# A causal convolution moved from a split between TensorE and VectorE to sixteen small TensorE tiles, in a fused retention and gated-linear-unit kernel

## The chip, the cores and the metric

The kernel runs on one core of one Trainium2 chip. The metric is device time in microseconds (us) of one execution. In the profile PE is TensorE (PEld its weight loads), DVE is VectorE, ACT is ScalarE, POOL is GpSimd and SP is SyncE, which here only issues DMAs.

## The reference

q, k and v are 8 batches x 8 heads x 576 positions x 64. First comes a retention layer, which is attention with a fixed decay in place of softmax; then a gated linear unit with a causal convolution as its gate:

```python
scores = scale * np.matmul(q, k.transpose(0, 1, 3, 2))
gamma = 1.0 - 2.0 ** (-5.0 - np.arange(H, dtype=np.float32))
Dmat = np.where(rel >= 0, gamma[:, None, None] ** rel[None, :, :], 0.0)
x = np.matmul(scores * Dmat[None], v)      # then heads side by side: (8, 576, 512)
for k in range(5):
    gate_pre += conv_w[k][None, None, :] * xp[:, k:k + S, :]   # xp: x with 4 zeros ahead
gate = 1.0 / (1.0 + np.exp(-gate_pre))
out = (gate * (x @ w_val)) @ w_out
```

The convolution is per channel: each of the 512 channels has its own five taps and is mixed with no other.

## The kernel before, in words

The sequence is cut into chunks of 128 positions, so a batch has four chunks and 64 positions left over. Two batches make a unit `u`; their leftovers are joined in one chunk of 2 x 64. That gives nine steps to a unit, and with four units 36 steps (L126 to L131).

A step `s` of attention is `load` (L135: q and k as float32 by SP's queue, v cast to bf16 on the way by POOL's queue), `cast` (L153: POOL multiplies q and k with the decay factors and rounds them to bf16), `transp` (L162: eight PE transposes into `tp`, then DVE copies `qt` and ACT copies `kt`), `scores` (L174: PE, then DVE multiplies with the mask into `am`), `state` (L193: PE, then ACT copies the running state `w`) and `attn_out` (L214: PE, then ACT copies the result into `xt`, the layer's x with channels on partitions, 512 channels as four tiles of 128, with four zero columns ahead). Loads run four steps ahead and casts two.

When a batch is done, `push_block` (L247) puts the gated unit's work for a block of positions on the list `work`: four `conv(d)`, one for each tile of channels; four `val(d)`; and one `outp(m)` for each 128 positions. There are 13 blocks: seven of 512 columns, two of 256, four of 2 x 64. The main loop (L320) takes three or four items off that list in each step, between the parts of attention; what is left runs after the last step. This gives the order in which the program is written; a scheduler then sets the final order on each engine, and each engine executes its own instructions in order.

`conv(d)` at L261 has two forms. For the channel tiles 0 and 1 (`PE_DT`), PE multiplies a 128x128 diagonal matrix of the weights of one tap with the shifted window of `xt`, ten times a tile: five taps, and for each the bf16 weight and its rounding remainder (L268). ACT applies the sigmoid from PSUM (L270). For the tiles 2 and 3, DVE does one multiply (L272) and four multiply-adds (L274), and ACT applies the sigmoid in place (L276). `val(d)` at L279 is four matmuls with `wval` (L284), then DVE multiplies with the gate into `zt` (L289). `outp(m)` at L291 is four matmuls with `wout` (L294), an ACT copy to `ob` (L297) and a DMA from SP's queue.

PSUM has eight banks: one for `tp` (pool `tpp`), two for the scores, one each for the attention output and the state, and three in the pool `glp`, which `cps`, `vps` and `ops` share in turn. SBUF pools: six buffers each for the loaded q, k and v, four each for their casts, four for `ob`.

Of the kernel before, what the change touches and what calls it, by code (L numbers as in the profile page):

```python
# [14 lines left out]
F32 = mybir.dt.float32  # L15
BF16 = mybir.dt.bfloat16
# [11 lines left out]
def kernel(  # L28
# [10 lines left out]
    nc = tc.nc  # L39
# [11 lines left out]
    lng = [math.log(1.0 - 2.0 ** (-5.0 - h)) for h in range(H)]  # L51
    PE_DT = (0, 1)

# [50 lines left out]
    wval = cst.tile([P, DT, DM], BF16)  # L104
    wout = cst.tile([P, DT, DM], BF16)
    diag = cst.tile([P, len(PE_DT), KC, 2, P], BF16)
    cwh = cst.tile([P, KC, DT], BF16)
    cwl = cst.tile([P, KC, DT], F32)

    def load_weights():  # L110
# [7 lines left out]
        nc.vector.tensor_copy(cwh, cw)  # L118
        nc.vector.tensor_tensor(cwl, cw, cwh, op=ALU.subtract)
        for n, dt_ in enumerate(PE_DT):  # L120
            for kk in range(KC):
                nc.vector.tensor_scalar_mul(diag[:, n, kk, 0, :], ident, cw[:, kk, dt_:dt_ + 1])
                nc.vector.tensor_scalar_mul(diag[:, n, kk, 1, :], ident, cwl[:, kk, dt_:dt_ + 1])

# [10 lines left out]
    def load(s):  # L135
        u, bb, c = steps[s]
        r = st.setdefault(s, {})
        qf = ld.tile([P, H, D], F32)
        kf = ld.tile([P, H, D], F32)
        vb = ld.tile([P, H, D], BF16)  # L140
        if bb is None:
            for x in range(2):
                b = 2 * u + x
                sl = slice(x * REM, (x + 1) * REM)
                for dst, src, eng in ((qf, q, nc.sync), (kf, k, nc.sync), (vb, v, nc.gpsimd)):
                    eng.dma_start(out=dst[sl], in_=src[b, :, NC * P:S, :].rearrange("h p d -> p h d"))
        else:
            b = 2 * u + bb
            for dst, src, eng in ((qf, q, nc.sync), (kf, k, nc.sync), (vb, v, nc.gpsimd)):
                eng.dma_start(out=dst, in_=src[b, :, c * P:(c + 1) * P, :].rearrange("h p d -> p h d"))  # L150
        r.update(qf=qf, kf=kf, vb=vb)

    def cast(s):  # L153
# [5 lines left out]
        nc.gpsimd.tensor_tensor(kb, r["kf"], fk[:, c, :].unsqueeze(2).to_broadcast([P, H, D]), op=ALU.mult)  # L159
        r.update(qb=qb, kb=kb)  # L160
# [86 lines left out]
    def push_block(u, bb, t0, n):  # L247
# [12 lines left out]

        def conv(d):  # L261
            gt = gl.tile(shape, F32, tag=f"g{N}", name="gt")
            if d in PE_DT:
                cp = glp.tile(shape, F32, tag="gps", name="cps")
                i = PE_DT.index(d)
                for kk in range(KC):
                    for p2 in range(2):
                        nc.tensor.matmul(cp, lhsT=diag[:, i, kk, p2, :], rhs=win(d, kk),  # L268
                                         start=(kk == 0 and p2 == 0), stop=(kk == KC - 1 and p2 == 1))
                nc.scalar.activation(gt, cp, AF.Sigmoid)  # L270
            else:
                nc.vector.tensor_scalar_mul(gt, win(d, 0), cw[:, 0, d:d + 1])  # L272
                for kk in range(1, KC):
                    nc.vector.scalar_tensor_tensor(gt, in0=win(d, kk), scalar=cw[:, kk, d:d + 1], in1=gt,  # L274
                                                   op0=ALU.mult, op1=ALU.add)
                nc.scalar.activation(gt, gt, AF.Sigmoid)  # L276
            g[d] = gt

        def val(d):  # L279
# [3 lines left out]
            for do in range(DT):  # L283
                nc.tensor.matmul(vp, lhsT=wval[:, do, d * P:(d + 1) * P], rhs=win(do, PAD),  # L284
                                 start=(do == 0), stop=(do == DT - 1))
# [17 lines left out]

        for d in range(DT):
            work.append((conv, d))
        for d in range(DT):
# [73 lines left out]
```

## Time and profile before

| what | value |
|---|---|
| median of 3 runs | 245.89 us (245.19 to 252.98) |
| the profiled execution's own time | 246.88 us |
| its span, first to last instruction | 245.2 us |
| mean granted PE clock | 0.95 |
| DMA, mean rate over the span | 140 GB/s |
| first matmul starts / last one ends | 18.1 / 240.5 us |

A row of a group reads: line, engine, operation, output<-inputs, shapes, count | busy us in all, mean ns of one | idle time of the engine just ahead of these, and what ended it. A row of waits reads: who waited <- for whom: us in all, times, longest. A row of the chain that ended last reads: start in us, us, what. A row of the timeline reads: start in us, us covered, what, count. A row of windows gives for a stretch its length, then busy us and instruction count for PE, PEld, DVE, ACT and POOL, then the granted clock, the DMA share and GB/s. Matmuls are pipelined, so the mean of one (its latency) is longer than the distance from one to the next.

### The profile page before, as it was taken

Reading aid. Unit: us, or ns where it says so; the run is one execution under the profiler, and the core shown is the slowest. Engines: PE = TensorE matmul, PEld = TensorE weight load, DVE = VectorE, ACT = ScalarE, POOL = GpSimd, SP = SyncE. Lnnn points to the kernel's source line nnn. Section 1 sums busy time; section 2 is a strip of 40 time slices with the busy share of each in tenths; the row PEclk is TensorE's granted clock in tenths of the full one; section 3 lists DMA queues with packets and bytes.
Section 4 is the critical chain, followed back from the end, with each engine's and each line's share of the span. In section 5 each row is a group of like instructions: output and inputs, shape, how many; then the busy total and the mean of one; then the engine's idle time right before and its main releaser. Section 6 shows DMA issues by size and latency. Waiting matters only on the chain.

```text
span 245.2 us, 4666 instructions
## 1 busy us (share of the span) xinstructions
PE 190.4 (78%) x1732; PEld 109.4 (45%) x1732; DVE 165.1 (67%) x323; ACT 109.8 (45%) x242; POOL 112.0 (46%) x126
## 2 busy tenths in 40 slices
PE   0007899259997989849978989759969999699592
PEld 0005564124554654415444745425534745356371
DVE  2073579994694582994895672992993854963991
ACT  2024465043634754534444755336445743533451
POOL 8129999624547392814444574706345620000000
PEclk9999999858999999989999999959999999979999
DMA  9999999903999999991997999935634901004032
GB/s 116 189 167 209 241 206 238 205 3 21 240 177 207 211 234 111 221 214 11 264 218 112 235 237 171 155 87 92 122 24 75 159 5 45 0 19 155 15 118 82
DMA packets 121478, 34.39 MB, mean 140 GB/s; under 512 B 115824, under 2 KB 116848, under 8 KB 121456
## 3 DMA queue, kind: packets, MB, share of 16 engines
q1 hardware_dynamic: 80256, 28.32, 47.4%
q0 software_dynamic: 38560, 5.77, 32.7%
q10 hardware_dynamic: 2640, 0.01, 0.7%
q8 instruction: 13, 0.21, 0.4%
q14 instruction: 9, 0.07, 0.1%
HBM read 30.42 MB, written 9.44 MB: 163 GB/s over the span
## 4 chain that ended last, share of the span: by engine, by line
PE 64%; DVE 18%; issue 7%; ACT 5%; POOL 4%; DVEq 0%; POOLq 0%
PE cps L268 15%; PE ops L294 14%; DVE gt L274 13%; PE vps L284 9%; PE tp L167 8%; PE o L226 7%; PE sc L183 6%; PE o L236 3%; DVE am L186 3%; ACT gt L276 2%; PE sts L202 2%; POOL vb L150 1%; ACT kt L171 1%; ACT w L209 1%; DVE gt L272 1%
## 5 line engine op out<-in xcount | busy, mean ns | idle before, releaser
L274 DVE SCALAR_TENSOR_TENSOR gt<-xt,cw,gt 128x512 f32<-128x512 bf16 (+2 forms) x104 | 67.2, 717 | 0.0
L158 POOL TENSOR_TENSOR qb<-qf,fq 128x512 bf16<-128x512 f32 x36 | 37.7, 1048 | 38.4 <-PE tp L167 19.3
L284 PE MATMUL vps<-xt,wval 128*128 128x512 bf16 (+2 forms) x208 | 39.8, 328 | 11.5 <-DVE zt L289 11.5
L186 DVE TENSOR_TENSOR am<-sc,mask_c 128x512 bf16<-128x512 f32 x64 | 41.2, 682 | 9.1 <-PE sc L183 8.9
L150 POOL DMA_DIRECT2D vb<-in_v_dram x32 | 29.6, 927 | 35.8 <-PE o L226 23.8
L170 DVE COPY qt<-tp 128x512 bf16<-128x512 bf16 x36 | 15.2, 421 | 42.3 <-PE tp L167 42.3
L268 PE MATMUL cps<-xt,diag 128*128 128x512 bf16 (+2 forms) x260 | 42.0, 313 | 0.0
L159 POOL TENSOR_TENSOR kb<-kf,fk 128x512 bf16<-128x512 f32 x36 | 38.3, 1066 | 6.3 <-issue 6.2
L294 PE MATMUL ops<-wout,zt 128*128 128x512 bf16 x144 | 38.3, 394 | 0.0
L167 PE MATMUL tp<-ident,qb 128*128 128x128 bf16 x144 | 17.2, 235 | 25.0 <-POOL qb L158 18.1
L241 ACT CAST xt<-o 128x512 bf16<-128x512 f32 x32 | 18.8, 586 | 35.3 <-PE o L236 29.4
L209 ACT CAST w<-sts 64x256 bf16<-64x256 f32 x64 | 23.4, 366 | 20.6 <-PE sts L202 20.0
L289 DVE TENSOR_TENSOR zt<-gt,vps 128x512 bf16<-128x512 f32 (+2 forms) x52 | 25.1, 516 | 8.6 <-PE vps L284 7.8
L226 PE MATMUL o<-am,vb 128*64 128x128 bf16 x288 | 23.5, 238 | 8.4 <-DVE am L186 8.3
L268 PEld LDWEIGHTS <-diag 128*128 128x128 bf16 x260 | 21.3, 97 | 16.3
L284 PEld LDWEIGHTS <-wval 128*128 128x128 bf16 x208 | 16.8, 99 | 22.5 <-issue 13.8
L171 ACT COPY kt<-tp 128x512 bf16<-128x512 bf16 x36 | 21.1, 587 | 12.7 <-DVE qt L170 12.5
L297 ACT COPY ob<-ops 128x512 f32<-128x512 f32 x36 | 20.5, 589 | 11.2 <-PE ops L294 9.0
L167 PEld LDWEIGHTS <-qb 128*128 128x128 bf16 x144 | 11.1, 103 | 31.5 <-POOL qb L158 18.5
L270 ACT ACTIVATE gt<-cps 128x512 f32<-128x512 f32 (+2 forms) x26 | 12.1, 466 | 21.3 <-PE cps L268 21.3
L183 PE MATMUL sc<-qt,kt 64*128 64x128 bf16 x288 | 21.3, 230 | 0.0
L226 PEld LDWEIGHTS <-vb 128*64 128x64 bf16 x288 | 12.7, 113 | 17.9 <-issue 9.9
(41 smaller groups left out, 145.5 us busy)
## 6 DMA issues: line engine op xcount, KB each, us to landing
qf<-in_q_dram SPq DMA_DIRECT2D x32, 256.0 KB, 4.9
kf<-in_k_dram SPq DMA_DIRECT2D x32, 256.0 KB, 4.7
out_dram<-ob SPq DMA_DIRECT2D x32, 256.0 KB, 2.6
vb<-in_v_dram POOLq DMA_DIRECT2D x32, 128.0 KB, 4.5
qf<-in_q_dram SPq DMA_DIRECT2D x8, 128.0 KB, 3.7
kf<-in_k_dram SPq DMA_DIRECT2D x8, 128.0 KB, 3.3
out_dram<-ob SPq DMA_DIRECT2D x8, 128.0 KB, 2.4
wval<-in_moe_w_val_dram POOLq DMA_DIRECT2D x1, 512.0 KB, 8.6
```

The lines of the kernel that those rows point to most:

```text
L150: eng.dma_start(out=dst, in_=src[b, :, c * P:(c + 1) * P, :].rearrange("h p d -> p h d"))
L158: nc.gpsimd.tensor_tensor(qb, r["qf"], fq[:, c, :].unsqueeze(2).to_broadcast([P, H, D]), op=ALU.mult)
L159: nc.gpsimd.tensor_tensor(kb, r["kf"], fk[:, c, :].unsqueeze(2).to_broadcast([P, H, D]), op=ALU.mult)
L167: nc.tensor.transpose(tp[:, n, hp, :], src[:, 2 * hp:2 * hp + 2, :].rearrange("p a d -> p (a d)"), ident)
L183: nc.tensor.matmul(sc[:, hp, :], lhsT=r["kt"][sl, hp, :], rhs=r["qt"][sl, hp, :], start=(hp == 0), stop=True, skip_group_check=True)
L186: nc.vector.tensor_tensor(am, sc, mk.unsqueeze(1).to_broadcast([P, HP, P]), op=ALU.mult)
L209: nc.scalar.copy(w[sl, :, hh * D:(hh + 1) * D], sp[sl, :, hh * D:(hh + 1) * D])
L226: nc.tensor.matmul(o[sl, hp, :], lhsT=r["vb"][:, 2 * hp + hh, :], rhs=r["am"][hh][:, hp, :], start=(hp == 0), stop=True, skip_group_check= ...
L268: nc.tensor.matmul(cp, lhsT=diag[:, i, kk, p2, :], rhs=win(d, kk), start=(kk == 0 and p2 == 0), stop=(kk == KC - 1 and p2 == 1))
L274: nc.vector.scalar_tensor_tensor(gt, in0=win(d, kk), scalar=cw[:, kk, d:d + 1], in1=gt, op0=ALU.mult, op1=ALU.add)
L284: nc.tensor.matmul(vp, lhsT=wval[:, do, d * P:(d + 1) * P], rhs=win(do, PAD), start=(do == 0), stop=(do == DT - 1))
L294: nc.tensor.matmul(op, lhsT=z[0][:, d, m * P:(m + 1) * P], rhs=wout[:, d, :], start=(d == 0), stop=(d == DT - 1))
```

## The change

**The convolution is wholly on PE, and one work item instead of four.** The array is used as 4 x 4 tiles of 32x32. Tile (r, c) holds the 32x32 diagonal of the channels 128c + 32r to 128c + 32r + 31: it reads the partitions 32r to 32r + 31 of channel tile c, and writes the partitions 32c to 32c + 31 of the PSUM tile `cps[r]`. For each of five taps and two weight parts there are 16 matmuls, one to a tile, so 160 to a block, each with a weight load of its own. Four `cps` are open at once; four sigmoids on ACT follow, one to a `cps`. DVE's multiplies are gone.

**Channels come out in another order**: `cps[r]` holds the channels 128c + 32r + x on partition 32c + x. So the columns of `wval` are permuted by four DVE copies at the start, and the rows of `wout` by loading it in four DMAs. The products of the diagonals are made by two wide DVE multiplies in place of twenty small ones.

**PSUM**: `tpp` is gone; `glp` has four buffers, and `tp` is one of its users.

**v** is loaded as float32 by SP's queue, 40 more DMAs there and 40 fewer on POOL's, and rounded to bf16 by a POOL copy in `cast`.

```diff
-    PE_DT = (0, 1)
+    Q = 32
+    NQ = P // Q
...
-    tpp = ctx.enter_context(tc.tile_pool(name="tpp", bufs=1, space=PS))
-    glp = ctx.enter_context(tc.tile_pool(name="glp", bufs=3, space=PS))
+    glp = ctx.enter_context(tc.tile_pool(name="glp", bufs=4, space=PS))
...
-        nc.gpsimd.dma_start(out=wval, in_=moe_w_val.rearrange("(do di) dp -> di do dp", di=P))
-        nc.gpsimd.dma_start(out=wout, in_=moe_w_out.rearrange("(do di) dp -> di do dp", di=P))
+        wtmp = cst.tile([P, DT, DM], BF16)
+        nc.gpsimd.dma_start(out=wtmp, in_=moe_w_val.rearrange("(do di) dp -> di do dp", di=P))
+        for do in range(DT):
+            nc.vector.tensor_copy(wval[:, do].rearrange("p r (c x) -> p r c x", x=Q),
+                                  wtmp[:, do].rearrange("p (c r x) -> p r c x", r=NQ, x=Q))
+        for c in range(DT):
+            nc.gpsimd.dma_start(
+                out=wout[c * Q:(c + 1) * Q],
+                in_=moe_w_out[c * P:(c + 1) * P, :].rearrange("(r x) n -> x r n", x=Q))
...
-        for n, dt_ in enumerate(PE_DT):
-            for kk in range(KC):
-                nc.vector.tensor_scalar_mul(diag[:, n, kk, 0, :], ident, cw[:, kk, dt_:dt_ + 1])
-                nc.vector.tensor_scalar_mul(diag[:, n, kk, 1, :], ident, cwl[:, kk, dt_:dt_ + 1])
+        nc.vector.tensor_tensor(idr, ident[:, 0:Q], ident[:, Q:2 * Q], op=ALU.add)
+        for i in range(2, NQ):
+            nc.vector.tensor_tensor(idr, idr, ident[:, i * Q:(i + 1) * Q], op=ALU.add)
+        shp = [P, KC * DT, Q]
+        for p2, w in ((0, cwh), (1, cwl)):
+            nc.vector.tensor_tensor(
+                diag[:, p2].rearrange("p k c x -> p (k c) x"),
+                idr.unsqueeze(1).to_broadcast(shp),
+                w.rearrange("p k c -> p (k c)").unsqueeze(2).to_broadcast(shp), op=ALU.mult)
...
-        vb = ld.tile([P, H, D], BF16)
+        vf = ld.tile([P, H, D], F32)
...
-            for dst, src, eng in ((qf, q, nc.sync), (kf, k, nc.sync), (vb, v, nc.gpsimd)):
+            for dst, src, eng in ((qf, q, nc.sync), (kf, k, nc.sync), (vf, v, nc.sync)):
...
+        vb = cs.tile([P, H, D], BF16)
+        nc.gpsimd.tensor_copy(vb, r["vf"])
...
-        tp = tpp.tile([P, 2, HP, P], BF16)
+        tp = glp.tile([P, 2, HP, P], BF16, tag="gps", name="tp")
...
+        def conv(_):
+            cps = [glp.tile(shape, F32, tag="gps", name="cps") for r in range(NQ)]
+            for kk in range(KC):
+                for p2 in range(2):
+                    for c in range(DT):
+                        for r in range(NQ):
+                            rs = slice(r * Q, (r + 1) * Q)
+                            nc.tensor.matmul(cps[r][c * Q:(c + 1) * Q], lhsT=diag[rs, p2, kk, c, :],
+                                             rhs=win(c, kk)[rs],
+                                             start=(kk == 0 and p2 == 0),
+                                             stop=(kk == KC - 1 and p2 == 1), skip_group_check=True,
+                                             tile_position=(r * Q, c * Q))
+            for r in range(NQ):
+                gt = gl.tile(shape, F32, tag=f"g{N}", name="gt")
+                nc.scalar.activation(gt, cps[r], AF.Sigmoid)
+                g[r] = gt
...
-                nc.tensor.matmul(vp, lhsT=wval[:, do, d * P:(d + 1) * P], rhs=win(do, PAD),
+                nc.tensor.matmul(vp, lhsT=wval[:, do, d, :], rhs=win(do, PAD),
...
-        for d in range(DT):
-            work.append((conv, d))
+        work.append((conv, 0))
```

How the instructions stand now, at three places. First DVE around the first two blocks, before (`am` is the masked score, `zt` the gated value, `gt` the gate):

```order
L186 TENSOR_TENSOR am<-sc,mask_c 128x512 x2
L170 COPY qt<-tp 128x512
L272 TENSOR_SCALAR gt<-xt,cw 128x512 x2
L274 SCALAR_TENSOR_TENSOR gt<-xt,cw,gt 128x512 x8
L186 TENSOR_TENSOR am<-sc,mask_c 128x512 x2
L289 TENSOR_TENSOR zt<-gt,vps 128x512 x3
```

The same place in the changed program (its L190 is the qt copy, L206 the mask multiply, L308 the gate multiply):

```order
L190 COPY qt<-tp 128x512
L206 TENSOR_TENSOR am<-sc,mask_c 128x512 x2
L308 TENSOR_TENSOR zt<-gt,vps 128x512 x3
L190 COPY qt<-tp 128x512
L308 TENSOR_TENSOR zt<-gt,vps 128x512
L190 COPY qt<-tp 128x512
```

The ten instructions of the convolution are gone, and nothing stands in their place between the mask multiplies and the gate multiplies.

Second, PE at the start of the second block's convolution in the changed program, with buffer numbers (L203 is a score matmul, L288 the convolution; 952 to 955 are the four `cps`):

```order
L203 MATMUL sc_1186<-qt_934,kt_935 128x128
L288 LDWEIGHTS diag_139
L288 MATMUL cps_952<-xt_259,diag_139 32x512
L288 LDWEIGHTS diag_139
L288 MATMUL cps_953<-xt_259,diag_139 32x512
L288 LDWEIGHTS diag_139
L288 MATMUL cps_954<-xt_259,diag_139 32x512
L288 LDWEIGHTS diag_139
L288 MATMUL cps_955<-xt_259,diag_139 32x512
```

Matmul and weight load alternate, and the four row groups follow each other, 160 times in one piece; before, 20 matmuls of 128x512 stood at this place. Behind this piece stand the attention output of the same step and, in the blocks of 512 columns, `val`.

Third, POOL after the weights' DMAs, before:

```order
L150 DMA vb_181<-in_v_dram 128x8x64
L150 DMA vb_187<-in_v_dram 128x8x64
L150 DMA vb_193<-in_v_dram 128x8x64
L158 TENSOR_TENSOR qb_197<-qf_144,fq_104 128x512
L159 TENSOR_TENSOR kb_198<-kf_145,fk_105 128x512
L158 TENSOR_TENSOR qb_201<-qf_179,fq_104 128x512
L159 TENSOR_TENSOR kb_202<-kf_180,fk_105 128x512
```

and in the changed program:

```order
L176 TENSOR_TENSOR qb_188<-qf_142,fq_101 128x512
L177 TENSOR_TENSOR kb_189<-kf_143,fk_102 128x512
L179 CAST vb_192<-vf_144 128x512
L176 TENSOR_TENSOR qb_194<-qf_170,fq_101 128x512
L177 TENSOR_TENSOR kb_195<-kf_171,fk_102 128x512
L179 CAST vb_198<-vf_172 128x512
```

The DMA issues of v are gone from POOL, and a copy of v stands behind the casts of q and k of each step.

More of the change, by code (lines that the diff above doesn't have):

```diff
@@ L51 @@
     lng = [math.log(1.0 - 2.0 ** (-5.0 - h)) for h in range(H)]
-    PE_DT = (0, 1)
+    Q = 32
+    NQ = P // Q
+    assert DT == NQ
     cst = ctx.enter_context(tc.tile_pool(name="cst", bufs=1))
@@ L103 @@
     cw = cst.tile([P, KC, DT], F32)
-    wval = cst.tile([P, DT, DM], BF16)
-    wout = cst.tile([P, DT, DM], BF16)
-    diag = cst.tile([P, len(PE_DT), KC, 2, P], BF16)
     cwh = cst.tile([P, KC, DT], BF16)
     cwl = cst.tile([P, KC, DT], F32)
+    idr = cst.tile([P, Q], BF16)
+    diag = cst.tile([P, 2, KC, DT, Q], BF16)
+    wval = cst.tile([P, DT, NQ, P], BF16)
+    wout = cst.tile([P, NQ, DM], BF16)
     def load_weights():
@@ L148, in load @@
             b = 2 * u + bb
-            for dst, src, eng in ((qf, q, nc.sync), (kf, k, nc.sync), (vb, v, nc.gpsimd)):
+            for dst, src, eng in ((qf, q, nc.sync), (kf, k, nc.sync), (vf, v, nc.sync)):
                 eng.dma_start(out=dst, in_=src[b, :, c * P:(c + 1) * P, :].rearrange("h p d -> p h d"))
-        r.update(qf=qf, kf=kf, vb=vb)
+        r.update(qf=qf, kf=kf, vf=vf)
     def cast(s):
@@ L159, in cast @@
         nc.gpsimd.tensor_tensor(kb, r["kf"], fk[:, c, :].unsqueeze(2).to_broadcast([P, H, D]), op=ALU.mult)
-        r.update(qb=qb, kb=kb)
+        vb = cs.tile([P, H, D], BF16)
+        nc.gpsimd.tensor_copy(vb, r["vf"])
+        r.update(qb=qb, kb=kb, vb=vb)
     def transp(s):
         r = st[s]
-        tp = tpp.tile([P, 2, HP, P], BF16)
+        tp = glp.tile([P, 2, HP, P], BF16, tag="gps", name="tp")
         for n, src in ((0, r["qb"]), (1, r["kb"])):
@@ L259, in push_block @@
         shape = [P, 2, n] if bb is None else [P, n]
[L261 to L277, printed above, removed]
+        def conv(_):
[14 more added lines that the diff above has]
+                g[r] = gt
         def val(d):
```

## The prediction

> **What bounds the kernel now.** I read the page first, then the waits, then the chain that ended last, then the clock by stretches.
>
> ```profile
> PE 190.4 (78%) x1732; PEld 109.4 (45%) x1732; DVE 165.1 (67%) x323; ACT 109.8 (45%) x242; POOL 112.0 (46%) x126
> PE 64%; DVE 18%; issue 7%; ACT 5%; POOL 4%; DVEq 0%; POOLq 0%
> PE tp L167 <- POOL qb L158: 18.1, 1, 18.1
> PE vps L284 <- DVE zt L289: 11.5, 4, 3.6
> PE o L226 <- DVE am L186: 8.3, 2, 7.6
> PE tp L167 <- ACT kt L171: 6.0, 6, 1.2
> PE sts L202 <- ACT w L209: 4.6, 8, 0.8
> ```
>
> TensorE (PE) is the bound: 190.4 us busy in a span of 245.2, 18.1 us of start before its first instruction, and some 32 us of waits behind that. The waits are where VectorE (DVE) or ScalarE (ACT) is late. The chain shows why:
>
> ```profile
> 36.26 3.34 DVE gt L272 x2
> 39.60 10.37 DVE gt L274 x7
> 51.22 0.61 DVE am L186
> 73.87 1.16 ACT gt L276 x2
> 75.05 0.59 ACT kt L171
> 99.36 6.97 DVE gt L274 x7
> 107.59 0.61 DVE zt L289
> ```
>
> DVE executes its half of a block's convolution (L272, L274) as one unbroken row of ten instructions. The mask multiply that attention waits for (51.22) and the gate multiply that the value matmuls wait for (107.59) stand behind it: 8.3 + 11.5 = 19.8 us of PE waits. On ACT the sigmoids of that half (73.87) stand ahead of the copy of kt, and PE's next transposes wait for it. Each long wait has a second price:
>
> ```profile
> 52.00:58.00 6.00, 6.00 (x32) 2.79 (x32) 4.43 (x8) 1.80 (x4) 1.99 (x2) 0.59 0.34 22
> 108.00:112.00 4.00, 3.76 (x18) 1.67 (x17) 3.55 (x8) 0.84 (x2) 0.17 (x1) 0.57 0.41 92
> 162.00:166.00 4.00, 4.00 (x17) 1.82 (x17) 3.30 (x7) 0.58 (x1) 0.39 (x1) 0.50 0.14 32
> 213.00:217.00 4.00, 3.84 (x24) 2.01 (x24) 3.85 (x8) 0.83 (x2) 0.00 (x0) 0.61 0.00 0
> ```
>
> The column before the last two is the granted clock: after four of these five waits PE restarts at about half. Lost: 6 x 0.41 + 4 x 0.43 + 4 x 0.50 + 4 x 0.39 = 7.7 us.
>
> **The change part by part.** Removed with certainty:
>
> ```profile
> L274 DVE SCALAR_TENSOR_TENSOR gt<-xt,cw,gt 128x512 f32<-128x512 bf16 (+2 forms) x104 | 67.2, 717 | 0.0
> L272 DVE TENSOR_SCALAR gt<-xt,cw 128x512 f32<-128x512 bf16 (+2 forms) x26 | 12.1, 506 | 0.1
> L268 PE MATMUL cps<-xt,diag 128*128 128x512 bf16 (+2 forms) x260 | 42.0, 313 | 0.0
> ```
>
> DVE loses 79.3 of 165.1 us, so its 19.8 us of PE waits go, and with them the restarts at half clock: -19.8 and -7.7. PE loses 42.0.
>
> Added on PE: 13 blocks x 160 = 2080 small matmuls, each with a weight load, in 130 groups of 16 (70 groups of 512 columns, 20 of 256, 40 of 128). Everything hangs on the price of a group. The nearest rows:
>
> ```profile
> 62.49 0.25 PE L226 MATMUL o<-am,vb 128*64 128x128 bf16 x2
> 62.49 0.41 PE L226 MATMUL o<-am,vb 128*64 128x128 bf16 x8
> 62.84 0.40 PE L236 MATMUL o<-qt,w 128*128 128x128 bf16 x4
> 63.07 0.39 PE L167 MATMUL tp<-ident,qb 128*128 128x128 bf16 x4
> 63.95 4.50 PE L268 MATMUL cps<-xt,diag 128*128 128x512 bf16 x20
> 68.39 0.41 PE L226 MATMUL o<-am,vb 128*64 128x128 bf16 x8
> 68.73 0.41 PE L233 MATMUL o<-qt,w 128*128 128x64 bf16 x8
> 68.97 0.39 PE L167 MATMUL tp<-ident,qb 128*128 128x128 bf16 x4
> 69.20 0.39 PE L167 MATMUL tp<-ident,kb 128*128 128x128 bf16 x4
> 69.52 0.41 PE L183 MATMUL sc<-qt,kt 64*128 64x128 bf16 x8
> 69.86 0.40 PE L202 MATMUL sts<-vb,kb 128*128 128x128 bf16 x4
> ```
>
> L226 works in two column halves of the array. Its first two matmuls together cover 0.25 us, as one alone does: they run at the same time. So tiles do overlap. Four full-array matmuls of 128 columns take 0.23 us (62.84 to 63.07), 58 ns each; eight L226 take 0.35, of which four such slots are 0.23 and about 0.1 is the change of array shape. L268 gives 222 ns for 512 columns (4.44 / 20).
>
> Lower bound: all 16 overlap wholly, a group costs one stream: 70 x 222 + 20 x 111 + 40 x 58 ns = 20.1 us. Upper bound: from 68.39 to 69.86 PE took 32 weight-and-matmul pairs in 1.47 us, 46 ns a pair, shape changes included. No row holds a faster rate over so many pairs, so I cannot exclude that PE takes in no pair faster than that: 2080 x 46 ns = 95.7 us. Shorter bursts do better: eight L233 in 0.24 us, 30 ns a pair. Since 14 ns (222 / 16) is needed for full overlap and 30 ns is only what eight full-width matmuls of 64 columns needed for streaming, I take a value between those two, 24 ns a pair: 130 x 16 x 24 ns = **+49.9 us**, for short blocks as for long ones. Shape changes around 13 blocks: +1.3.
>
> The Trainium skill, TensorE: Matmul & The Clock Gate, "Wait — 56ns, not 53.3ns?", says that matmuls start no closer than about 25 ns however short they are; by that alone the convolution would be 52 us and the run 233.6. The x2 row above disagrees for two tiles, and no run here shows a long stream.
>
> New waits. A convolution now takes all four buffers of the PSUM pool that also holds tp, vps and ops. Its first matmuls wait until ACT has emptied the last tp or ops (0.59 as in the kt row), and val(0) waits for the first of four sigmoids in a row on ACT (1.16 / 2 = 0.58 each). Behind conv stand the attention output and often the next scores, about 0.5 us of cover. All of PE's work is queued behind either wait. I take 0.4 us at either end of a block: 13 x 0.8 = +10.4; bounds 0 and the case below. Of the 10.6 us of waits for ACT (kt, w) I let 5 go: sigmoids no longer wait for DVE, but four stand in one row.
>
> Off the path:
>
> ```profile
> L158 POOL TENSOR_TENSOR qb<-qf,fq 128x512 bf16<-128x512 f32 x36 | 37.7, 1048 | 38.4 <-PE tp L167 19.3 <-DVE fq L83 10.2 <-issue 7.1
> L150 POOL DMA_DIRECT2D vb<-in_v_dram x32 | 29.6, 927 | 35.8 <-PE o L226 23.8 <-PE tp L167 11.8 <-issue 0.2
> q1 hardware_dynamic: 80256, 28.32, 47.4%
> q0 software_dynamic: 38560, 5.77, 32.7%
> ```
>
> GpSimd loses a DMA issue of 0.93 us a step and gains a copy of 128x512, not shown before: between nothing and the 1.05 us of the two-input multiply, I take 0.75. GpSimd has 54% idle, so nothing follows. SP issues 40 more loads; out DMAs queue behind them, and the four ob buffers cover that. A software packet took 0.327 x 245.2 x 16 / 38560 = 33 ns of an engine, a hardware packet 23: with 36864 packets moved, the DMA work falls from 196 to some 173 us. It hides while the span stays above that.
>
> The start:
>
> ```profile
> 12.39 0.18 DVE L118 CAST cwh<-cw 128x20 bf16<-128x20 f32 x1 [10.08 <-DMA cw<-in_moe_conv_w_dram]
> 16.73 0.18 DVE L83 TENSOR_SCALAR fq<-fq 128x40 f32<-128x40 f32 x1
> L123 DVE TENSOR_SCALAR diag<-ident,cwl 128x128 bf16<-128x128 bf16 x10 | 2.5, 248 | 0.0
> ```
>
> The first cast of q waits for fq, which stands behind twenty diagonals, most of those 4.3 us. Three short adds and two products of 640 columns replace them, perhaps 1.8 us: -1.5. The wval copies stand behind fq.
>
> **Sum:** 245.2 - 42.0 + 49.9 + 1.3 - 19.8 - 7.7 - 5 + 10.4 - 1.5 = 230.8 us of span. The profiled execution took 246.88, 1.7 more than its span, and 1.0 more than the median of 245.89: 230.8 + 1.7 - 1.0 = **231.5 us**.
>
> **The rivals.** *Full overlap.* A group costs one stream; the sum falls by 29.8, to 201.7, and DMA then has 173 of 200 us and costs a little: 203. For it: the x2 row. Against: sixteen tiles take in 32 instructions every 222 ns, and no row shows such a rate. The Trainium skill, TensorE: Matmul & The Clock Gate, "Part 3: Packing small matmuls — row/col tiling", has 16 tiles of 512 columns at 10.6 times one after another, with starts some 4 ns apart; that would give this time, and the x2 row agrees for two tiles.
>
> *Pairs come too slowly (slower).* PE takes in pairs at a fixed pace in the middle of each convolution, whatever their size; 2.08 us for each ns of a pair. From 31 ns on the kernel is no faster than before, from 33 it is over 2% slower; at 46 it is 231.5 + 45.8 = 277. For it: the 46 ns stretch, and blocks of 128 columns, which cost 1.2 us today (20 x 58 ns) and would cost 7.4. Against: the stretch contains shape changes and streams that account for most of it.
>
> *The wait moves to PSUM.* If PE waits for all four sigmoids of a block before it goes on, seven long blocks cost 2.3 us, two half ones 1.6, four short ones 1.1, plus 0.4 at each start: 29 in place of 10.4, so 250, no change. For it: one pool for everything. Against: val(1) needs only the second sigmoid, and a val takes 0.9 us, longer than a sigmoid.
>
> **How the numbers follow.** My forecast (18 to 30 ns a pair, 219 to 244) has 0.48, full overlap 0.18, slow pairs 0.22, PSUM 0.12. A difference of 2% is about what a measurement of this kernel can tell. Faster: 0.48 + 0.18 less the upper edge of the forecast, 0.64. Slower: 0.22. Same: 0.14. The range runs from full overlap to 38 ns a pair: 203 to 260; the forecast's own is 219 to 244.
>
> **What would show it.** Right: L288 groups at about 24 x 16 = 384 ns, also in 128-column blocks; PE's waits for zt and am near nothing; no stretch at half clock after the start; DVE near 90 us. Wrong: groups at 222 ns or above 500; PE waiting on the sigmoids for over 20 us; the DVE waits gone but PE waiting for loads.

## The result, and the profile after

| | before | after |
|---|---|---|
| median of 4 runs each, on one chip | 248.54 us (245.19 to 252.98) | 220.38 us (219.09 to 222.32) |
| profiled execution / its span | 246.88 / 245.2 us | 219.09 / 217.4 us |
| mean granted PE clock, from its first record on (at 29.6 and 40.6 us) | 0.950 | 0.978 |

The ratio is 0.898, with a 95% interval of 0.887 to 0.910: faster; it compares the fast executions alone, since two of the four before took over 1.5% longer than the fastest. The span lost 27.8 us. Read it first from the page of the changed kernel: the busy times, the shares of the chain that ended last, the DMA queues, and the convolution's row.

```profile
PE 174.5 (80%) x3532; PEld 110.5 (51%) x3552; DVE 92.4 (43%) x182; ACT 106.7 (49%) x242; POOL 98.7 (45%) x125
q1 hardware_dynamic: 117760, 37.76, 79.1%
q0 software_dynamic: 1104, 1.05, 3.0%
q8 instruction: 27, 0.44, 0.9%
PE 71%; issue 13%; ACT 7%; POOL 5%; DVE 2%; ACTq 0%; POOLq 0%
L288 PE MATMUL cps<-xt,diag 32*32 32x512 bf16 (+2 forms) x2080 | 31.0, 315 | 9.9 <-issue 5.6
```

DVE fell to 92.4 us and left the chain (18% before, 2% now). PE has twice the instructions and is busy 15.9 us less. The convolution takes 31.0 us, where 42.0 on PE and 79.3 on DVE were. But "issue" rose from 7% to 13% of the chain: time in which PE waits for nothing that the profile shows. PE's waits say the same:

```profile
PE tp L187 <- POOL qb L176: 19.6, 3, 18.9
PE cps L288 <- issue: 5.6, 3, 2.8
PE cps L288 <- ACT ob L316: 2.4, 4, 0.7
PE vps L303 <- ACT gt L295: 2.4, 3, 1.6
PE vps L303 <- issue: 2.1, 3, 1.4
PE sts L222 <- issue: 1.2, 1, 1.2
PE cps L288 <- ACT kt L191: 1.2, 4, 0.6
PE cps L288 <- ACT xt L261: 0.7, 2, 0.3
PE ops L313 <- issue: 0.2, 1, 0.2
```

No wait for DVE is left. The first row is the start (18.9 us). ACT keeps PE for 2.4 + 2.4 + 1.2 + 0.7 = 6.7 us. The issue rows add up to 9.1 us, and PE had no such row before. Where they lie is seen in the timeline of PE around the second, third and fifth convolution of the changed kernel (the time in brackets is the idle time ahead of a row):

```profile
59.12 2.13 PE L288 MATMUL cps<-xt,diag 32*32 32x512 bf16 x134
64.08 0.73 PE L288 MATMUL cps<-xt,diag 32*32 32x512 bf16 x26 [2.83 <-issue]
...
77.50 1.22 PE L288 MATMUL cps<-xt,diag 32*32 32x128 bf16 x121 [0.67 <-ACT ob L316]
80.96 0.29 PE L288 MATMUL cps<-xt,diag 32*32 32x128 bf16 x18 [2.23 <-issue]
...
108.88 2.43 PE L288 MATMUL cps<-xt,diag 32*32 32x512 bf16 x160 [0.33 <-ACT xt L261]
```

The last row is a convolution that nothing disturbs: 160 matmuls of 512 columns in 2.43 us, with 2.05 us from the first start to the last. That is ten streams of some 0.22 us: all sixteen tiles stream at the same time. The rows above show PE stopping in the middle of a block, 26 and 18 matmuls before its end. Both stops are followed by a stretch at about half clock; here are the stretches behind each stop (the column before the last two is the clock; its records put the half clock at 64.49 to 67.91 and at 81.56 to 84.97 us):

```profile
64.00:68.00 4.00, 3.70 (x47) 1.88 (x49) 0.27 (x1) 2.54 (x5) 2.65 (x3) 0.57 0.96 214
81.00:85.00 4.00, 4.00 (x61) 3.45 (x62) 1.73 (x4) 2.34 (x8) 2.34 (x3) 0.57 1.03 237
```

That costs another 2 x 4 x 0.43 = 3.4 us. So three questions: is the gain the convolution's, and which part of it; what are the stops; and what is the start worth.

### The profile page after: what moved, and what is told of

Read it like the earlier page. It is cut to its first block, busy times and chain, and to the rows that moved or that the text cites. A ratio compares the mean times of both kernels' runs of the same rounds, so it can differ in the third digit from the quotient of the medians.

```text
span 217.4 us, 8277 instructions
## 1 busy us (share of the span) xinstructions
PE 174.5 (80%) x3532; PEld 110.5 (51%) x3552; DVE 92.4 (43%) x182; ACT 106.7 (49%) x242; POOL 98.7 (45%) x125
## 4 chain that ended last, share of the span: by engine, by line
PE 71%; issue 13%; ACT 7%; POOL 5%; DVE 2%; ACTq 0%; POOLq 0%
PE vps L303 15%; PE ops L313 13%; PE cps L288 13%; PE o L246 8%; PE tp L187 8%; PE sc L203 5%; PE sts L222 4%; PE o L256 4%; ACT kt L191 2%; DVE qt L190 2%; ACT w L229 2%; ACT gt L295 2%; POOL qb L176 1%; POOL kb L177 1%; ACT ob L316 1%
## 5 line engine op out<-in xcount | busy, mean ns | idle before, releaser
L206 DVE TENSOR_TENSOR am<-sc,mask_c 128x512 bf16<-128x512 f32 x64 | 41.8, 683 | 20.8 <-PE sc L203 20.4
L308 DVE TENSOR_TENSOR zt<-gt,vps 128x512 bf16<-128x512 f32 (+2 forms) x52 | 26.8, 523 | 46.8 <-PE vps L303 40.5
L303 PE MATMUL vps<-xt,wval 128*128 128x512 bf16 (+2 forms) x201 | 37.3, 321 | 4.9 <-ACT gt L295 2.4
L288 PE MATMUL cps<-xt,diag 32*32 32x512 bf16 (+2 forms) x2080 | 31.0, 315 | 9.9 <-issue 5.6
L313 PE MATMUL ops<-wout,zt 128*128 128x512 bf16 x131 | 35.0, 380 | 0.8 <-issue 0.2
L295 ACT ACTIVATE gt<-cps 128x512 f32<-128x512 f32 (+2 forms) x52 | 20.0, 471 | 26.9 <-PE cps L288 26.9
L187 PE MATMUL tp<-ident,qb 128*128 128x128 bf16 x144 | 16.0, 237 | 19.6 <-POOL qb L176 19.6
L288 PEld LDWEIGHTS <-diag 32*32 32x32 bf16 x2080 | 22.9, 88 | 16.8 <-issue 14.7
L190 DVE COPY qt<-tp 128x512 bf16<-128x512 bf16 x36 | 15.2, 423 | 37.4 <-PE tp L187 37.2
L179 POOL CAST vb<-vf 128x512 bf16<-128x512 f32 x36 | 22.0, 610 | 9.8 <-DMA vf<-in_v_dram 5.7
L187 PEld LDWEIGHTS <-qb 128*128 128x128 bf16 x144 | 10.9, 105 | 24.0 <-POOL qb L176 20.0
L261 ACT CAST xt<-o 128x512 bf16<-128x512 f32 x32 | 18.9, 591 | 8.2 <-PE o L256 7.8
L246 PE MATMUL o<-am,vb 128*64 128x128 bf16 x288 | 21.1, 239 | 0.2
L203 PE MATMUL sc<-qt,kt 64*128 64x128 bf16 x288 | 20.4, 233 | 0.0
L313 PEld LDWEIGHTS <-zt 128*128 128x128 bf16 x144 | 13.0, 98 | 14.3 <-issue 1.5
```

The costliest lines, as they stand in the source:

```text
L187: nc.tensor.transpose(tp[:, n, hp, :], src[:, 2 * hp:2 * hp + 2, :].rearrange("p a d -> p (a d)"), ident)
L203: nc.tensor.matmul(sc[:, hp, :], lhsT=r["kt"][sl, hp, :], rhs=r["qt"][sl, hp, :], start=(hp == 0), stop=True, skip_group_check=True)
L206: nc.vector.tensor_tensor(am, sc, mk.unsqueeze(1).to_broadcast([P, HP, P]), op=ALU.mult)
L246: nc.tensor.matmul(o[sl, hp, :], lhsT=r["vb"][:, 2 * hp + hh, :], rhs=r["am"][hh][:, hp, :], start=(hp == 0), stop=True, skip_group_check= ...
L288: nc.tensor.matmul(cps[r][c * Q:(c + 1) * Q], lhsT=diag[rs, p2, kk, c, :], rhs=win(c, kk)[rs], start=(kk == 0 and p2 == 0), stop=(kk == KC ...
L303: nc.tensor.matmul(vp, lhsT=wval[:, do, d, :], rhs=win(do, PAD), start=(do == 0), stop=(do == DT - 1))
```

## The experiments

**Theory A**: the gain comes from the convolution alone, and needs both DVE off PE's path and tiles that overlap. **Rival B**: the new load path for v gives it, or loads pace the kernel. **Rival C**: to free DVE is enough. **Theory D**: the stops are PE waiting for its own instructions. They come to the chip through a queue of their own (q8) in packets of 16384 bytes, 27 of them for some 7100 PE instructions (13 for some 3460 before); that fits a page of 256 to a packet, the first one loaded ahead. **Rival E**: the stops belong to their place (PSUM, data, clock).

**1. The convolution's half alone** (v loaded as before).

```diff
-        vf = ld.tile([P, H, D], F32)
+        vb = ld.tile([P, H, D], BF16)
-                for dst, src, eng in (..., (vf, v, nc.sync)):
+                for dst, src, eng in (..., (vb, v, nc.gpsimd)):
-        nc.gpsimd.tensor_copy(vb, r["vf"])
```

> The convolution's half of the change alone; v comes as before, cast to bf16 on the way by GpSimd's DMA queue. Theory A (the gain is the convolution: DVE off PE's path and sixteen tiles that overlap): about 220 us, 216 to 227; convolution rows at 31 us, DVE at 92 us busy, the waits of PE for zt and am gone. Rival B (the load path gives the gain, DMA work of 196 us paces the kernel): 235 us or more, PE waiting for loads or for GpSimd by more than 15 us after the start.

Measured: 221.72 us (220.51 to 223.39), ratio to before 0.891 (0.874 to 0.909), beside 0.898 for the whole change. The convolution rows take 30.5 us. Theory A holds: the gain is here, as far as these runs can tell.

**2. The other half alone**, on the kernel before.

> The load path's half alone, on the kernel before: v as float32 by SP's queue and rounded on GpSimd, convolution as before. Theory A: no change, 244 to 252 us beside 248 for the kernel before, the waits for zt, am and kt as before. Rival B: 225 to 235 us.

Measured: 269.37 us (269.01 to 271.73), ratio 1.082 (1.066 to 1.098). Neither theory had this: alone, the new load path costs 8%. PE's waits in this kernel (L185 is the scores, L173 the copy of kt, L188 the mask multiply):

```profile
PE sc L185 <- ACT kt L173: 24.3, 11, 6.5
PE tp L169 <- POOL qb L158: 19.7, 1, 19.7
PE o L228 <- DVE am L188: 14.8, 13, 4.5
```

Before, the two largest of such waits were 11.5 (zt) and 8.3 (am). The order on DVE is another: behind the ten convolution rows of the first block the mask multiplies had come next, and now the copy of qt does (52.17 us); in the second block copies of qt stand between the rows (71.26 and 77.97). ACT's kt and PE's scores wait for these copies, and the mask multiplies follow. So the same DVE rows stand ahead of more of PE's work. That this order is the whole cause is read from the waits, and was not tested alone. With those rows gone (runs 1 and the changed kernel, 221.7 and 220.4) the load path makes no difference that these runs can tell.

**3. DVE freed, but no small tiles**: the kernel before with all four channel tiles as 128x128 diagonals.

```diff
-    PE_DT = (0, 1)
+    PE_DT = (0, 1, 2, 3)
```

> The kernel before with all four channel tiles on PE as 128x128 diagonals: DVE is off the convolution, but there are no small tiles. Theory A (both are needed): PE's convolution rows go from 42 to 84 us, the waits for DVE (19.8 us) and the restarts at half clock (7.7 us) go: 248.5 + 42 - 27.5 - 5 = 258 us, 250 to 266. Rival C (it is enough that DVE is off PE's path; the overlap of the tiles matters little): 221 to 235 us.

Measured: 252.63 us (248.97 to 254.62), ratio 1.006 (0.999 to 1.013). Rival C falls: what is gained by freeing DVE is eaten by 41 us more on PE.

```profile
PE 214.0 (85%) x1965; PEld 127.1 (50%) x1992; DVE 103.7 (41%) x213; ACT 111.0 (44%) x242; POOL 111.9 (44%) x126
L268 PE MATMUL cps<-xt,diag 128*128 128x512 bf16 (+2 forms) x512 | 83.3, 314 | 0.6 <-issue 0.2
PE tp L167 <- ACT kt L171: 11.7, 1, 11.7
```

PE's convolution is 83.3 us as expected, and the waits for DVE are gone but for 0.8. It came out below my 258 although a wait of 11.7 us at the start was new (forty diagonals on DVE, see the last section): the other PE rows take 214.0 - 83.3 = 130.7 us, 17.7 less than before, where I had allowed 7.7 for the clock (0.995 here in its records, which begin at 51.8 us). Without the wait of 11.7 us the run would be near 241, by subtraction, and still outside Rival C's numbers. From this kernel to the changed one PE's convolution loses 52.3 us, and the run 32.

**4. The pages shifted**: the changed kernel with 64 matmuls ahead of everything.

```diff
+    dm = glp.tile([P, P], F32, tag="gps", name="dm")
+    for i in range(64):
+        nc.tensor.matmul(dm, lhsT=ident, rhs=ident, start=True, stop=True)
```

> The changed kernel with 64 matmuls of the identity ahead of everything on PE, while PE is idle at the start; they write a PSUM tile that nothing reads. They shift every later PE instruction by 128 places, half of a 16 KB page of 256 instructions. Theory D (the stops without a releaser in the convolutions are PE waiting for its instructions, one page of look-ahead, a page some 4 to 5 us after the one before it): the stops leave the second and third convolution (2.8 and 2.2 us at 61 and 79 us) and turn up where two page ends now fall in or just ahead of a convolution: in the 1st, 5th, 6th, 7th, 11th and 13th, 1 to 3 us each; each ends 1.3 to 1.5 us after the end of a packet of the instruction queue; time 219 to 229 us. Rival E (the stops belong to their place: PSUM, data, the clock): they stay in the second and third convolution; time 219 to 222 us.

Measured: 224.59 us (222.32 to 225.89). The second convolution and the eleventh, in this kernel's timeline:

```profile
61.21 2.43 PE L292 MATMUL cps<-xt,diag 32*32 32x512 bf16 x160
...
192.02 1.72 PE L292 MATMUL cps<-xt,diag 32*32 32x256 bf16 x152
196.02 0.30 PE L292 MATMUL cps<-xt,diag 32*32 32x256 bf16 x8 [2.28 <-issue]
```

The second now runs undisturbed in 2.43 us, and the third has no such stop in it either. The eleventh, undisturbed in the changed kernel (1.79 us), stops for 2.3 us. New stops of 0.84 and 0.54 us stand in the fifth and seventh, and of 2.54 and 1.34 us just behind the eighth and tenth. Those blocks are as they were, with more PE instructions ahead of them: Rival E falls. The places count out as pages do. In the changed kernel the stops of the issue rows from 0.4 us up stand behind 1211, 1721, 2995, 3506, 4525 and 7076 recorded PE instructions (weight loads and matmuls), in run 4 behind 2996, 4017, 4781, 5802, 6312 and 6821: all apart by whole multiples of about 255, with a few instructions missing from the records. The edit put other parts of the program at these counts and left the counts alone. Each time PE had gone through the last 255 in under 5 us; other such places have no stop. My list of places was too simple: the first, sixth and thirteenth have no such stop in them (ahead of the thirteenth stands one of 1.02 us; the first ran at half clock here, where PE takes longer over a page). In these two traces each of these stops ends 1.2 to 1.5 us after a packet of q8 does: in the changed kernel the packet of 61.31 to 62.61 us stands ahead of the restart at 64.08, that of 78.32 to 79.47 ahead of 80.96, that of 209.14 to 210.07 ahead of 211.37.

**5. Half the matmuls**: the changed kernel without the weights' rounding remainders.

```diff
-                for p2 in range(2):
+                for p2 in range(1):
```

> The changed kernel without the rounding remainders of the weights: 80 pairs to a convolution in place of 160 (the gate is then computed from bf16 weights alone). Theory D (stream plus waits for instructions): the convolution rows fall from 31 to about 15 us, and the stops without a releaser (some 9 us inside and just behind convolutions) go, since 160 instructions rarely cross two pages: 220.4 - 15.5 - 8 = 197 us, 193 to 204. Rival B (the load path paces: 179 us of DMA work, GpSimd waits 41 us for loads): 208 us or more, and PE waits for GpSimd in place of the convolution.

Measured: 224.16 us (218.95 to 225.09), no gain, and the convolution rows still 31.0 us. By the numbers that is Rival B's side, but not its mechanism, since PE's waits for GpSimd after the start are as small as before. One convolution of it shows why (L187 is the transposes):

```profile
138.43 0.61 PE L288 MATMUL cps<-xt,diag 32*32 32x512 bf16 x15
138.97 0.40 PE L187 MATMUL tp<-ident,kb 128*128 128x128 bf16 x4
139.30 0.63 PE L288 MATMUL cps<-xt,diag 32*32 32x512 bf16 x22
140.50 1.26 PE L288 MATMUL cps<-xt,diag 32*32 32x512 bf16 x43 [0.57 <-ACT kt L191]
```

The scheduler gave the fourth PSUM buffer to tp first, so the last 43 matmuls wait until ACT has copied kt out of it. The run tested the order more than the number; that the issue waits all but vanished (0.9 us of 9.1) is all that it says on Theory D. Runs 9 and 10 repeat it.

**6. Fewer loads.**

```diff
-        vf = ld.tile([P, H, D], F32)
+        if s % 2 == 0 or bb is None:
+            vf = ld.tile([P, H, D], F32)
+        else:
+            vf = st[s - 1]["vf"]
...
-            for dst, src, eng in ((qf, q, nc.sync), (kf, k, nc.sync), (vf, v, nc.sync)):
+            for dst, src, eng in ((qf, q, nc.sync), (kf, k, nc.sync), (vf, v, nc.sync))[:3 if s % 2 == 0 else 2]:
```

> The changed kernel with 16 of the 32 full loads of v left out (an odd step uses the v of the step before, so its output is another): about 16 x 1024 packets x 23 ns / 16 = 24 us less DMA work. Theory A (loads do not pace this kernel): 217 to 222 us. Rival B: 205 to 213 us.

Measured: 213.79 us (212.89 to 215.85), 6.6 less than the changed kernel: outside Theory A's numbers, and 0.8 above Rival B's. The loads do cost something. PE's second and third convolution here, and a stretch behind each:

```profile
59.75 0.63 PE L291 MATMUL cps<-xt,diag 32*32 32x512 bf16 x26 [1.70 <-issue]
...
74.78 0.29 PE L291 MATMUL cps<-xt,diag 32*32 32x128 bf16 x18 [1.77 <-issue]
```

```profile
60.00:64.00 4.00, 3.93 (x59) 2.07 (x35) 1.43 (x3) 2.54 (x5) 2.09 (x2) 1.00 0.83 178
75.00:79.00 4.00, 4.00 (x85) 3.27 (x68) 2.49 (x7) 2.48 (x8) 2.93 (x5) 1.00 0.99 192
```

The stops are at the same places, but 1.70 and 1.77 us long in place of 2.83 and 2.23, and the clock stays at 1.00 behind them, where it had fallen to 0.57. That is 1.6 + 3.4 = 5.0 us. It is not the whole account. Ahead of both stops this run is already 3.2 us earlier (the second convolution starts at 55.91, against 59.12), and PE's slow pace at the start ends at about 32 us in place of 41 (see the last section). And later stops are longer: one of 1.85 us at 131.73 has a stretch at half clock behind it, and all the issue rows together come to 8.1 us, beside 9.1.

```profile
131.50:134.90 3.40, 3.17 (x8) 1.21 (x8) 0.98 (x2) 0.00 (x0) 0.00 (x0) 0.50 1.05 233
```

PE still does not wait for GpSimd after the start, so the loads do not pace the attention. That they lengthen the stops, since a page of instructions travels through the same DMA engines, would fit these two, but is not shown: in run 1, which loads all of v, the same two are 1.63 and 2.49 us long.

**7. The start freed.**

```diff
-    nc.vector.tensor_copy(pos, pos_i)
+    nc.gpsimd.tensor_copy(pos, pos_i)
...
-    nc.vector.tensor_scalar_mul(fq, fq, scale)
+    nc.gpsimd.tensor_scalar_mul(fq, fq, scale)
...
+    with tc.issue_after(iexp.ins):
+        load_cw()
     cast(0)
+    with tc.issue_after(st[0]["last"].ins):
+        load_wval()
...
+            with tc.issue_after(st[s]["iam"].ins):
+                if s == 1:
+                    prep_diag()
+                else:
+                    prep_wval((2 * s - 4, 2 * s - 3))
```

> The changed kernel with its start freed: positions and the scaling of fq on GpSimd, the conv weights' DMAs on ScalarE's queue behind the exponentials, the DMAs of wval and wout behind the first and the third cast, and VectorE's work on diag and wval behind the mask multiplies of the second to fourth step. q, k and v of the first step land at 3.6, 5.2 and 12.1 us today, so the first cast of q need not wait for fq until 17.6. Theory F (the start is 10 us of pure loss): the first matmul at 6 to 8 us in place of 18.9, the first convolution at 24 to 30 in place of 39, and 205 to 214 us in all. Rival G (loads pace the first steps, what is gained at the start is lost before the second block): 216 us or more.

Measured: 212.33 us (209.78 to 213.18), ratio to before 0.852 (0.843 to 0.861); Theory F holds in the sum. First the changed kernel's DVE and ACT at the start, then PE and GpSimd with the start freed:

```profile
14.28 0.18 DVE L131 CAST cwh<-cw 128x20 bf16<-128x20 f32 x1 [11.97 <-DMA qf<-in_q_dram]
14.59 0.16 DVE L76 CAST pos<-pos_i 128x5 f32<-128x5 int32 x1
15.04 0.21 ACT L82 ACTIVATE fq<-pos 128x5 f32<-128x5 f32 x1 [9.97 <-DVE pos L77]
17.36 0.18 DVE L84 TENSOR_SCALAR fq<-fq 128x40 f32<-128x40 f32 x1
```

```profile
7.54 0.61 PE L196 MATMUL tp<-ident,qb 128*128 128x128 bf16 x4 [7.54 <-POOL qb L184]
...
3.80 0.34 POOL L84 TENSOR_SCALAR fq<-fq 128x40 f32<-128x40 f32 x1 [1.44 <-ACT fq L82]
```

A cast of the convolution's weights (14.28; the row names another DMA, but what it reads is cw) stood ahead of the cast of the positions on DVE, and everything hung on that: the exponentials, fq, and GpSimd's first cast. The first matmul came 11.4 us earlier. The first convolution came only 6.9 us earlier (32.25), not the 9 to 15 that I had expected, since GpSimd's casts now wait for the loads of the first steps (kb until 16.50, 3.0 us for kf) and PE's slow pace at the start still lasts until about 28 us.

**8. The same matmuls in another order**: all ten of one tile, then the next tile.

```diff
-            for kk in range(KC):
-                for p2 in range(2):
-                    for c in range(DT):
-                        for r in range(NQ):
+            for c in range(DT):
+                for r in range(NQ):
+                    for kk in range(KC):
+                        for p2 in range(2):
```

> The changed kernel with the two pairs of loops of the convolution exchanged: the ten matmuls of one 32x32 tile follow each other, then comes the next tile; the same instructions in another order. Theory A (the gain is that sixteen tiles stream at the same time): next to none of it is left, a pair costs its own stream, 70 x 16 x 222 + 20 x 16 x 111 + 40 x 16 x 58 ns = 322 us in place of 20: 480 to 540 us. Rival H (small matmuls are cheap by themselves, or TensorE takes them out of order): below 260 us.

Measured: 424.23 us (one run). The convolution's row and one block of it:

```profile
L288 PE MATMUL cps<-xt,diag 32*32 32x512 bf16 (+2 forms) x2080 | 241.3, 348 | 0.7 <-ACT xt L261 0.7
128.44 22.04 PE L288 MATMUL cps<-xt,diag 32*32 32x512 bf16 x160
```

Same instructions, 241.3 us in place of 31.0: what makes them cheap is that neighbours in the row go to different tiles. Rival H falls. My 322 was too much, since an undisturbed block took 100 streams of 0.217 us, not 160: to every ten matmuls the trace has six starts some 0.2 us apart and four within 20 ns of another. So the last four of one tile's ten run beside the first four of the next tile's, as far as the pattern of starts tells.

**9 and 10. Half the matmuls again, and its control.** In both, nothing may stand between the matmuls of a convolution; 10 has all 160, 9 has 80.

```diff
+            with tc.tile_critical():
                 for kk in range(KC):
```

> As the run without the rounding remainders, but the scheduler may put nothing between the 80 pairs of a convolution (there it had put transposes after the first 15, into the fourth PSUM buffer, and 512 columns took 3.0 to 4.5 us for five groups). Theory D (what is left of the convolution's cost is streams plus waits for instructions): about 1.3 us for 512 columns, the stops without a releaser gone, clock 0.97 or more: 193 to 205 us. Rival B (loads pace the kernel from about there): 210 us or more.

> Control for the run before: the changed kernel with the remainders, and nothing put between the 160 pairs of a convolution. Both theories: like the changed kernel, 217 to 225 us; stops without a releaser stay, 5 us or more in all.

Measured: 271.08 us for 9, 304.77 for 10. Both miss every theory's numbers, and the control says why: the closed section itself costs some 84 us. PE waits ahead of each section, the scores wait for kt twenty times, and the clock falls to 0.82. Only the pair can be compared, 80 matmuls (first fence) against 160 (second):

```profile
PE sc L203 <- ACT kt L191: 23.5, 20, 1.3
PE cps L289 <- issue: 3.3, 1, 3.3
```

```profile
PE sc L203 <- ACT kt L191: 23.2, 20, 1.3
PE cps L289 <- issue: 14.5, 7, 4.4
```

Everything around is alike, and the stops fall from 14.5 us in seven places to 3.3 in one. That one stands ahead of the twelfth convolution, where run 10 has one of 3.1 us as well; inside the convolutions six stops of 11.4 us in all become none. All seven 512-column blocks of run 9 take 1.74 us from first start to last, alike within 5 ns (at about half pace: a matmul takes 602 to 629 ns, against 371 to 385 in the undisturbed block); those of run 10 take from 3.65 to 5.72. This is Theory D's other half: fewer instructions to a block, no stop in it.

**11. Start freed, half the matmuls, closed sections.**

> The freed start, without the rounding remainders and with whole convolutions. Theory D and F add up: 212 less 15 to 23 us: 188 to 199. Rival B: the 179 us of DMA work begin to pace it, PE waits for GpSimd and GpSimd for loads: 201 or more.

Measured: 270.88 us (261.60 to 271.86). That is far from Theory D and F together, but it has the closed sections too, and says nothing beyond run 9.

**12. Start freed, and two fewer convolutions.**

```diff
-        N = 2 * n if bb is None else n
+        N = 4 * n if bb is None else n
...
+            nc.vector.tensor_copy(xls[u // 2][:, :, h0:h0 + 2, :], xt[:, :, :, NC * P:PAD + S])
...
-            push_block(u, None, NC * P, REM)
+            if u % 2 == 1:
+                push_block(u, None, NC * P, REM)
```

> The freed start, and the 2 x 64 leftover positions of two units put together in one block of 256 columns, so there are 11 convolutions in place of 13 (a VectorE copy keeps the leftover columns of a unit). A 128-column convolution takes 2.1 us, a 256-column one 1.5: -2 x 2.1 - 2 x 0.6 = -5, less for the copies and other pages: 206 to 210 us, beside 212 for the freed start alone. Rival (other places of the page ends, a longer tail): 212 or more.

Measured: 208.44 us (206.49 to 210.44), ratio to before 0.822 (0.814 to 0.831). It leaves nothing out, and is the fastest of all the kernels here. The rival's mechanism is at work as well: with 640 PE instructions fewer, PE's issue waits are 10.7 us, beside 10.1 with the freed start alone, at other places.

## Why the prediction was right, and where it was not

The time came out at 220.4 against 231.5 forecast, inside the range and inside the forecast's own (219 to 244). That it fell inside is in part luck: errors of -29.5 us in all (the convolution -20.2, the old ACT waits -5.6, the new waits -3.7) met errors of +16.1 (the stops 9.1, PE's other rows 2.8, the start 2.3, the rest 1.9).

| term of the sum | forecast, us | measured, us |
|---|---|---|
| convolution on PE, old rows out | -42.0 | -42.0 |
| convolution on PE, new rows in (and shape changes) | +49.9 + 1.3 | +31.0 |
| PE's waits for DVE | -19.8 | -19.8 |
| PE's other rows, half clock for the most part | -7.7 | -4.9 |
| old waits for ACT (kt, w) | -5 | -10.6 |
| new waits for PSUM and sigmoids | +10.4 | +6.7 |
| start | -1.5 | +0.8 |
| stops for instructions | not in it | +9.1 |
| the rest (tail, small waits) | not in it | +1.9 |
| sum | -14.4 | -27.8 |

- **DVE off the path** held to the digit: no zt or am wait is left, DVE is at 92.4 us (about 90 was said).
- **The price of a group** is the step that failed: "I take a value between those two, 24 ns a pair". By its own test the forecast is wrong here and the rival of full overlap right: a group of 512 columns took 228 ns (2.05 us from the first start to the last, nine groups later), and the rows 31.0 us, not 49.9 and 1.3 for shape changes. The 30 ns that I leaned on were the streaming time of full-width matmuls and no limit on what PE takes in; the x2 row, two matmuls in the time of one, was the better witness. The limit that I had looked for does exist, but lower: the undisturbed 256-column block (1.51 us from first start to last, 160 pairs) shows 9.5 ns a pair, where sixteen tiles with 111 ns of stream would allow 7. The Trainium skill, TensorE: Matmul & The Clock Gate, "Part 3: Packing small matmuls — row/col tiling", was right about starts some 4 ns apart: this trace has them 3 to 4 ns apart in the first group of the undisturbed block of 512 columns, and mostly 8 to 9 ns in the blocks of 256. The same page's 25 ns between starts does not hold for neighbours in different tiles.
- **Why full overlap gave 220 and not the rival's 203**: the stops (9.1), the half clock behind two of them (3.4), the start (2.3 later than forecast), a first block at half pace, and blocks of 256 and 128 columns limited by what PE takes in. What I named there as the next bound, DMA, did not show as one: with less loading (run 6) the kernel is 6.6 us faster, but PE waits for no load after the start, and the issue rows lose only 1.0 us.
- **PE's other rows** lost 4.9 us in place of 7.7. Half clock was left: the two stretches behind stops, and a start at about half pace until 40.6 us, where it had ended at 29.6 before. What the longer slow start costs was not measured.
- **New waits**: 6.7 us in place of 10.4, and PE waited for sigmoids 2.4 us at most, so the rival of the PSUM wait did not come. The longest of these, 1.6 us at 139.01, is probably a stop too: it stands behind 4017 recorded PE instructions, as a stop of run 4 does, and 1.5 us behind a packet of q8, while the first of the four sigmoids had ended at 137.35. The old ACT waits all went, not half of them: without DVE's rows ACT was no longer late.
- **Start**: the direction was wrong. I counted DVE's work ahead of fq and not what the first of it waits for: cw lands late, and DVE's row begins at 14.28 us where it had begun at 12.39.
- **The load path** at nothing was right in this kernel (0.61 us a copy where I took 0.75; 179 us of DMA work where I reckoned 173). Run 2 shows the condition: with DVE's convolution rows still there, the same edit costs 8%, as its waits have it by the order that it sets.

What stays open: why a page arrives as late as it does (the stop's end, 1.2 to 1.5 us after the packet's, is seen and not explained), why other places where pages follow as fast have no stop, and how run 6's gain divides between an earlier end of the slow start, the stops and the clock.

## What to carry to other kernels

Small matmuls on different tiles of the array overlap almost wholly at 512 columns if neighbours in the instruction row go to different tiles (31 us against 241 for the same instructions in another order), so price a group by one stream and by the number of pairs at some 9 ns (this kernel's figure), whichever is more. Then count PE's instructions: bursts of several hundred in two microseconds ran into stops that no wait names, and these are moved by any edit ahead of them, so a small difference between two versions may be theirs. And look at what the first instruction behind the start really waits for: here it was a cast needed only by the convolution at 39 us, and the run that moved it, with the rest of the start's work, gained 8.

## What the runs showed of the hardware that was not expected

- **PE can wait for its own instructions.** One convolution is 320 PE instructions in 2.1 to 2.4 us. PE stopped up to 2.8 us at places some 255 recorded instructions apart, or a multiple of that, where it had gone through the last 255 in under 5 us. With 128 instructions put ahead the stops fell on other convolutions at the same counts (run 4), and with half the instructions none was left inside a convolution (run 9). The Trainium skill, Runtime: NRT & Kernel Launch, "Instruction fetch mechanics", has the fetch hidden by the pace at which instructions issue; in these runs it was not.
- **A stop's length alone does not decide over the clock.** Behind stops of 2.83 and 2.23 us PE restarted at 0.57, and behind 1.70 and 1.77 us at 1.00 (run 6). But behind 1.85 us in run 6 it ran at 0.50, and behind 2.54 us in run 4 at 1.00, in the row below. What decides is open. In the clock's records of these traces, a stretch at 0.50 that ends before the kernel does lasts 3.4 us or a multiple of it.

```profile
153.10:157.10 4.00, 3.95 (x29) 2.17 (x31) 2.39 (x5) 0.59 (x1) 2.96 (x3) 1.00 0.94 204
```

- **Busy is not the same as warm.** In run 8, with one or two of the sixteen tiles streaming without a pause, the clock fell to 0.50 in two of the seven long blocks (first row). In run 4, 64 matmuls in the first 7 us, then idle, did not spare PE a start at 0.50, from 12 to 46 us (second row):

```profile
170.00:200.00 30.00, 30.00 (x120) 10.71 (x119) 0.00 (x0) 0.60 (x1) 3.12 (x3) 0.50 0.37 64
```

```profile
12.00:40.00 28.00, 19.14 (x164) 11.57 (x164) 14.29 (x31) 10.29 (x35) 21.10 (x26) 0.50 1.26 215
```

- **The clock column is silent where it has no record.** In the changed kernel the records begin at 40.6 us, and a window ahead of that reads 1.00. The score matmuls say otherwise: those of the first 40 us took 303 ns on average, those between 85 and 133 us 219 ns, so PE started at a slow pace here as well. By the same measure and the first record it ended at about 30 us in the kernel before, 41 in the changed one, 32 in run 6 and 28 in run 7.

```profile
L203 PE MATMUL sc<-qt,kt 64*128 64x128 bf16 x40 | 4.8, 303 | 0.0
```

```profile
L203 PE MATMUL sc<-qt,kt 64*128 64x128 bf16 x80 | 4.8, 219 | 0.0
```

- **A short DVE instruction can take many times its length beside GpSimd.** In run 3 the diagonals that DVE makes (128x128, 0.24 us each until then) took 1.08 and up to 3.75 us once GpSimd was at its first casts, and 0.24 us again from 29.52 on, when GpSimd was idle:

```profile
17.11 0.25 DVE L123 TENSOR_SCALAR diag<-ident,cwl 128x128 bf16<-128x128 bf16 x1
...
18.55 1.08 DVE L122 TENSOR_SCALAR diag<-ident,cw 128x128 bf16<-128x128 bf16 x1
...
24.85 3.75 DVE L123 TENSOR_SCALAR diag<-ident,cwl 128x128 bf16<-128x128 bf16 x1
```
